# Two of the four opening x tiles move from ScalarE's DMA queue to SyncE's, behind the first two weights

## The chip, the cores and the metric

The kernel runs on one core of a Trainium2 chip. The metric is the device time of one execution in microseconds (us), as the median of several runs. A core has TensorE (PE; its weight loads are shown apart as PEld), VectorE (DVE), ScalarE (ACT), GpSimd (POOL) and SyncE (SP), each with its own instruction stream, and 16 DMA engines that move data between HBM and the on-chip memory. A DMA is issued by an engine's instruction stream; here nearly all are issued by SyncE, and a few by ScalarE.

## The reference

```python
def _A_ref(x, wqkv, wo):          # S = 2048, D = 1024, H = 32 heads
    W, dil = 8, 2
    qkv = (x @ wqkv).reshape(B, S, 3, H, Dh).transpose(2, 0, 3, 1, 4)
    q, k, v = qkv[0], qkv[1], qkv[2]
    # position s attends to s, s-2, ..., s-14 (those that exist)
    ...
    return o.transpose(0, 2, 1, 3).reshape(B, S, D) @ wo

def _B_ref(x, w1, b1, w2, b2):    # F = 3584
    h = jnp.maximum(x @ w1 + b1, 0)
    return (h * h) @ w2 + b2

x = A_x
x = x + _A_ref(_layernorm(x), A_wqkv, A_wo)
x = x + _B_ref(_layernorm(x), B_w1, B_b1, B_w2, B_b2)
x = x + _A_ref(_layernorm(x), A_wqkv, A_wo)
x = x + _B_ref(_layernorm(x), B_w1, B_b1, B_w2, B_b2)
```

Two layers of a dilated sliding-window attention and a dense block with a squared ReLU, both on a layernorm of x, all in bfloat16.

## The kernel before

The 2048 rows are cut into four blocks of 512, a block into four tiles of 128 rows (`tl` 0 to 3). With two layers that makes eight units `u`. The stages of a unit are methods that add operations to a plan: `SA` loads the four x tiles, normalises and transposes them into `xnA`; `SQ` (or `SQ7`, with seven products in place of eight) multiplies by the q, k and v weights; `S2` is the attention, `SW` the output product, `SF1` and `SF2` the dense block. The operations are not emitted as they are added. `Plan.schedule` simulates the engines with a cost for each operation and gives every engine an order, steered by priorities and by three lists of seeds (`ORDER`), and `emit` writes the operations out in that order. Each engine then runs its own stream strictly in order, and waits where an operand is not there.

The opening is unit 0. In `SA(0)` the tiles are taken in the order `ORD = (0, 1, 3, 2)`. Tiles 0 and 1 (x0 and x1 in this text) are issued by SyncE, tiles 3 and 2 (x3 and x2) by ScalarE, since `XACT = (3, 2)`. So "third and fourth" are x3 and then x2.

- x0, x1 and x2 go through `ln_first`: statistics on VectorE (L801, L803), the factor on ScalarE (L794, L795), normalising on VectorE (L798), transposing on TensorE (L817) and a copy into `xnA` by VectorE or ScalarE (L822). For x0 and x1 the transpose and the copy are done in two halves, the first half's copy on VectorE and the second's on ScalarE.
- x3 (`LNA = (3,)`) goes through `ln`: sums on ScalarE (L756 and L760), normalising on VectorE (L769). Its first pass is placed after the factors of x0 and x1 (`after=rst`).
- `keep_clock` (L1559) adds matmuls on constants or on the first normalised tile (`pk`, `pj`) that nobody reads; they occupy TensorE while data are on their way.
- `SQ(0, "kq")` loads the k and q weights in eight pieces of 512 KB on SyncE, alternating k and q; w0 is the first piece of k, w1 the first of q, w2 the second of k, and so on. Its first 16 chunks of matmuls (L909) use only tiles 0 and 1 (256 columns), so they need x0 and x1 transposed and one weight piece each. Tiles 2 and 3 are used later.

On SyncE the order is x0, x1, the eight weight pieces, and then x tiles of the next block (`xt`). Every DMA raises one of eight semaphores when it lands; they are given out in turn, over all queues together, and a DMA that gets a semaphore in use is issued only when the DMA before it on that semaphore has landed.

Of the kernel before, what the change touches and what calls it, by code (L numbers as in the profile page):

```python
# [62 lines left out]
XH = False  # L63
T2 = True
N0 = 4667
XP = -4e5
TAIL = True
CPT = ("xn3",)
# [71 lines left out]
class Plan:  # L140
# [160 lines left out]
    def shift(self, seeds):  # L301

        n = N0 or len(self.ops)
        for s in seeds:
# [21 lines left out]
    def emit(self, place):  # L326
        ndep, left = [o.ndep for o in self.ops], {b: b.left for o in self.ops for b in o.bufs}
        for i, seeds in enumerate(ORDER or [[]]):
            if i:
                for s, o in self.timed:  # L330
                    o.prio = s
                for o, n in zip(self.ops, ndep):
                    o.ndep = n
                for b, n in left.items():
                    b.left, b.slot = n, None
            (self.reshift if i else self.shift)(seeds)
            order, self.timed = self.schedule()
        for o in order:
            for b in o.bufs:
                if b.tile is None:  # L340
                    b.tile = place(b)
            o.fn()

class _Kernel:
# [73 lines left out]
    def place(self, b):  # L418
        pool = self.psum if b.cls == "ps" else self.arena
        return pool.tile(b.shape, b.dt, name=b.tag, tag=f"{b.cls}.{b.slot}", bufs=1)  # L420
# [8 lines left out]
    def dma(self, out, src, r, w, mb, prio=None, after=(), name="dma", cast=None, lat=None, eng="SP", dur=None):  # L429
        def fn():  # L430
            o = out()
            (self.nc.sync if eng == "SP" else self.nc.scalar).dma_start(o if cast is None else o.bitcast(cast), src())
        return self.p.add(eng, dur or 0.08, fn, r, w, self.nxt() if prio is None else prio, after, mb=mb, name=name, lat=lat)

    def par_tile(self, par_ap, t):
# [411 lines left out]
    def SA(self, u):  # L847
# [7 lines left out]
        for tl in ORD if u == 0 else range(4):  # L855
            t = b * 4 + tl
            x, xv = self.load_x(layer, t, after, tag="x0" if u == 0 else "xt", prio=PR1 if u == 1 else (XP if tl in XACT else -1e6) if u == 0 else None,
                                eng="ACT" if u == 0 and tl in XACT else "SP")
# [807 lines left out]
```

## Time and profile before

| | |
|---|---|
| median of 3 runs | 1132.15 us (1131.62 to 1132.54) |
| the profiled execution | 1131.64 us, of which the span from the first to the last instruction is 1129.8 us |
| TensorE busy | 1119.7 us, 99% of the span |
| VectorE busy | 993.9 us, 88% |
| ScalarE busy | 816.6 us, 72% |
| DMA, mean over the span | 321 GB/s |
| mean granted TensorE clock | 1.000 |

The times in the views are us from the span's start. A row of the timeline has start, duration, engine, line, operation with output and inputs, count, and in brackets the idle time of the engine before it and what ended it. A "q" behind an engine's name (SPq, ACTq) is its instruction stream issuing a DMA. In the chain of waits a row has start, length and what the time went to. The table by stage gives for each stretch its length, the busy time (and number of instructions) of each engine, the granted TensorE clock, the share of time that the DMA engines were busy, and GB/s.

### The profile page before, as it was taken

The numbers are of one execution on the slowest core, as the hardware profiler recorded it, in microseconds if no ns is written. First come the engines' busy times: TensorE is split into PE (matmuls) and PEld (weight loads), VectorE is DVE, ScalarE is ACT, GpSimd is POOL, SyncE is SP. The second block draws the span as 40 slices with busy tenths as digits, with TensorE's granted clock in tenths as the row PEclk, the third lists the DMA queues.
The fourth block names the chain that finished last, engine by engine and source line by source line (L and its number), as shares of the span: only waits on it lengthen the run. The fifth ranks groups of instructions, "written<-read, shape, count | busy, mean of one in ns | idle before, by whom it ended". The sixth has DMA issues, their size and how long they took to land.

```text
span 1129.8 us, 20640 instructions
## 1 busy us (share of the span) xinstructions
PE 1119.7 (99%) x7866; PEld 771.5 (68%) x7912; DVE 993.9 (88%) x1530; ACT 816.6 (72%) x1627; POOL 1.8 (0%) x8
## 2 busy tenths in 40 slices
PE   8999999999999999999999999999999999999998
PEld 6645764678846887468864788557884678845864
DVE  8999999999897999959999699996999889996341
ACT  7647897568975799667994669847798477943871
POOL 0000000000000000000000000000000000000000
PEclk9999999999999999999999999999999999999999
DMA  9957889999999986999779998899969999679981
GB/s 355 310 183 240 272 286 334 304 361 383 367 340 382 365 352 245 351 419 355 284 284 317 406 346 319 296 348 374 384 252 333 363 348 394 237 291 339 345 296 68
DMA packets 137021, 362.34 MB, mean 321 GB/s; under 512 B 67418, under 2 KB 68570, under 8 KB 116570
## 3 DMA queue, kind: packets, MB, share of 16 engines
q1 hardware_dynamic: 136490, 360.43, 91.4%
q8 instruction: 62, 1.02, 0.4%
q10 hardware_dynamic: 432, 0.59, 0.1%
q14 instruction: 37, 0.30, 0.1%
HBM read 314.84 MB, written 31.46 MB: 307 GB/s over the span
## 4 chain that ended last, share of the span: by engine, by line
PE 83%; ACT 8%; DVE 5%; DMA 2%; issue 1%; SPq 0%; DVEq 0%; ACTq 0%
PE X L673 22%; PE X L1409 14%; PE Z L673 11%; PE Z L1409 7%; PE Y L673 6%; PE pq L909 5%; PE py L495 4%; PE Y L1409 4%; PE py L1105 3%; PE X L1176 3%; DVE P L979 2%; ACT r L1344 1%; PE Z L1176 1%; ACT rr L1350 1%; DVE P L971 1%
## 5 line engine op out<-in xcount | busy, mean ns | idle before, releaser
L673 PEld LDWEIGHTS <-w 128*128 128x128 f16 (+1 forms) x4904 | 479.6, 98 | 70.4 <-DMA w<-sqv 0.5
L1409 PEld LDWEIGHTS <-r 128*128 128x128 f16 x1162 | 113.7, 98 | 133.4 <-issue 1.5
L1409 PE MATMUL X<-w,r 128*128 128x512 f16 (+1 forms) x763 | 174.1, 379 | 0.6 <-ACT X L508 0.2
L971 DVE TENSOR_TENSOR P<-q,k 128x2048 f16<-128x2048 f16 x128 | 153.4, 1220 | 0.6 <-ACT q L914 0.4
L673 PE MATMUL X<-T,w 128*128 128x256 f16 x1224 | 152.6, 273 | 0.0
L1050 DVE TENSOR_TENSOR pr<-pb,v 128x4096 f16<-128x4096 f16 x64 | 146.0, 2294 | 0.5
L979 DVE TENSOR_TENSOR P<-P,P 128x2048 f16<-128x2048 f16 x110 | 133.5, 1216 | 0.1
L1344 ACT ACTIVATE r<-rr 128x1024 f16<-128x1024 f16 x110 | 122.7, 1133 | 0.5 <-DVE rr L1340 0.4
L1057 DVE TENSOR_TENSOR pr<-pr 128x2048 f16<-128x2048 f16 (+1 forms) x128 | 118.7, 949 | 0.0
L673 PE MATMUL X<-TA,w 128*128 128x256 f16 x864 | 107.9, 273 | 0.0
L909 PE MATMUL pq<-xnA,w 128*128 128x256 f16 (+1 forms) x512 | 86.1, 326 | 1.5 <-ACT k L914 0.8
L606 ACT COPY Y<-X 128x512 f32<-128x512 f32 x115 | 70.1, 609 | 21.0 <-PE X L673 18.3
L1323 ACT CAST y<-Z 128x512 f16<-128x512 f32 x110 | 68.2, 639 | 7.0 <-PE Z L673 6.4
L909 PEld LDWEIGHTS <-w 128*128 128x128 bf16 x512 | 49.9, 98 | 33.1 <-issue 2.1
L1327 DVE TENSOR_TENSOR rr<-u,y 128x512 f16<-128x512 f16 x110 | 45.5, 419 | 26.4 <-ACT u L1313 15.6
L1350 ACT ACTIVATE rr<-Y,b1T 128x256 f16<-128x256 f32 x110 | 53.6, 525 | 4.4 <-PE Y L673 3.6
L673 PE MATMUL X<-xnB,w 128*128 128x256 f16 x440 | 56.0, 273 | 0.0
L673 PE MATMUL Y<-xnB,w 128*128 128x256 f16 x440 | 56.0, 273 | 0.0
L624 ACT CAST u<-X 128x512 f16<-128x512 f32 x72 | 41.8, 585 | 19.2 <-PE X L673 19.2
L1078 ACT CAST yxo<-X 128x512 f16<-128x512 f32 x27 | 15.6, 587 | 55.4 <-PE X L1409 55.4
L1350 ACT ACTIVATE rr<-X,b1T 128x256 f16<-128x256 f32 x110 | 54.7, 546 | 1.2 <-PE X L673 1.1
L628 ACT CAST yq<-Z 128x512 f16<-128x512 f32 x72 | 42.0, 586 | 17.5 <-PE Z L673 17.0
(170 smaller groups left out, 1689.2 us busy)
## 6 DMA issues: line engine op xcount, KB each, us to landing
w<-sw SPq DMA_DIRECT2D x49, 1024.0 KB, 9.7
w<-tw SPq DMA_DIRECT2D x56, 896.0 KB, 6.7
w<-in_B_w_dram SPq DMA_DIRECT2D x42, 896.0 KB, 5.6
w<-in_B_w_dram SPq DMA_DIRECT2D x35, 1024.0 KB, 11.1
w<-in_A_wqkv_dram SPq DMA_DIRECT2D x32, 1024.0 KB, 10.7
w<-sqv SPq DMA_DIRECT2D x24, 1024.0 KB, 11.4
w<-in_B_w_dram SPq DMA_DIRECT2D x28, 512.0 KB, 6.7
w<-sk SPq DMA_DIRECT2D x12, 1024.0 KB, 8.5
```

The lines of the kernel that those rows point to most:

```text
L606: self.p.add("ACT", act(512), lambda: self.nc.scalar.copy(Y[:], X[:]), [(X, 0)], [(Y, 0)], UP, name="u")
L673: nc.tensor.matmul(bank[:, a, :], lw[:, k, a * 128:(a + 1) * 128], rhs(k), start=(start and k == 0 and a == 0), stop=(k == 3), skip_group_ ...
L909: nc.tensor.matmul(pq[:, t0 * HB:t1 * HB], w[:, c0 // 2 % 2, kd // 4, kd % 4, c0 % 2 * 128:c0 % 2 * 128 + 128], xnT[:, 2 * t0:2 * t1, kd, ...
L971: nc.vector.tensor_tensor(cur[:], q[:, c, None, hb * HB:(hb + 1) * HB].to_broadcast([128, W, HB]), _win_ap(k[:, c, :], HALO + hb * HB, HB) ...
L979: nc.vector.tensor_tensor(other[:], other[:], cur[:], ALU.add)
L1050: p.add("DVE", dve(4096), lambda pr=pr, ch=ch: nc.vector.tensor_tensor(pr[:], pb[:].unsqueeze(1).to_broadcast([128, 2, W, HB]), _win_ap2(v ...
L1057: nc.vector.tensor_tensor(dst, pr[:, :, 0:n, :], pr[:, :, n:2 * n, :], ALU.add)
L1323: p.add("ACT", act(512), lambda: nc.scalar.copy(y[:], bank[:]), [(bank, 0)], [(y, 0)], 1.5, name="y")
L1327: p.add("DVE", dve(512), lambda: nc.vector.tensor_tensor(r[:, :, m, :], us[i][:], y[:], ALU.add), [(us[i], 0), (us[i], 1), (y, 0)], [(r, ( ...
L1344: p.add("ACT", 0.955, lambda: nc.scalar.activation(out=r2[:, f:f + 2, :].rearrange("p a t -> p (a t)"), in_=r[:].rearrange("p a m t -> p ( ...
L1350: p.add("ACT", 0.36, lambda a=a: nc.scalar.activation(out=r[:, a, 0, :], in_=bank[:, a, :], func=ACTF.Relu, bias=self.b1T[:, f + a:f + a + ...
L1409: nc.tensor.matmul(banks[q][:, lo:hi], left(jj, q), w[:, j, lo:hi], start=(start and jj == 0), stop=(jj == h - 1), skip_group_check=True)
```

## The change

In the finished order the two x loads that belong to ScalarE are taken out and put back right behind the second weight load, and every x load is issued by SyncE. The plan itself is made as before, with its costs and its order, so all other instructions keep their order on each engine. `B2AT` stands at 0.0 and does nothing. Since semaphores are given out in the order of emission, the first eight DMAs now take them in the order x0, x1, w0, w1, x3, x2, w2, w3 (before: x0, x1, x3, w0, x2, w1, w2, w3).

```diff
+B2AT = 0.0
+XSP = 2
...
             (self.reshift if i else self.shift)(seeds)
             order, self.timed = self.schedule()
+        at = {o: s for s, o in self.timed}
+        if B2AT:
+            b2 = next(o for o in order if o.name == "b2")
+            order.remove(b2)
+            order.insert(next(i for i, o in enumerate(order) if at[o] >= B2AT), b2)
+        if XSP:
+            late = [o for o in order if o.name == "x" and o.eng == "ACT"]
+            ws = [o for o in order if o.name == "w"]
+            order = [o for o in order if o not in late]
+            i = order.index(ws[XSP - 1]) + 1
+            order[i:i] = late
         for o in order:
             for b in o.bufs:
...
-            (self.nc.sync if eng == "SP" else self.nc.scalar).dma_start(o if cast is None else o.bitcast(cast), src())
+            (self.nc.sync if eng == "SP" or XSP and name == "x" else self.nc.scalar).dma_start(o if cast is None else o.bitcast(cast), src())
```

## The prediction

> **What bounds the kernel now.** I began with the page's first lines and with the table of busy time by stage, cut at the points where TensorE stands still: 11.22 us (the end of the opening), 36.23 us and 1120 us.
>
> ```profile
> span 1129.8 us, 20640 instructions
> PE 1119.7 (99%) x7866; PEld 771.5 (68%) x7912; DVE 993.9 (88%) x1530; ACT 816.6 (72%) x1627; POOL 1.8 (0%) x8
> ```
>
> ```profile
> core 0: us, PE busy (x) PEld busy (x) DVE busy (x) ACT busy (x) POOL busy (x), PEclk, DMA share, GB/s
> 0.00:11.22 11.22, 8.17 (x39) 3.54 (x40) 7.44 (x22) 5.66 (x13) 1.76 (x8) 1.00 0.85 322
> 11.22:36.23 25.01, 24.19 (x225) 21.25 (x225) 23.33 (x26) 18.58 (x50) 0.00 (x0) 1.00 1.08 338
> 36.23:1120.00 1083.77, 1080.72 (x7559) 742.49 (x7605) 961.84 (x1481) 790.79 (x1563) 0.00 (x0) 1.00 0.92 323
> ```
>
> TensorE is the bound. It is idle for 11.22 - 8.17 = 3.05 us in the opening, 0.82 us in the next 25 us and 1083.77 - 1080.72 = 3.05 us in all the rest up to 1120 us. The change touches only the opening, so the question is when the first real matmuls start, and whether a shift there reaches the end. The second view is the chain of waits, read forward from its start:
>
> ```profile
> 1.26 4.43 DMA x<-in_A_x_dram
> ...
> 5.71 1.30 DVE st L801 x2
> ...
> 7.81 1.05 ACT xn L756 x2
> ...
> 9.08 0.48 ACT xnA L822
> 9.56 1.14 ACT xn L760 x2
> 10.70 0.48 ACT xnA L822
> ...
> 11.22 2.34 PE pq L909 x20
> ```
>
> It runs: load of x1 (the tile tl = 1), its statistics on VectorE, then ScalarE alone from 7.8 to 11.2 us, then the first long row of matmuls. ScalarE's piece is the first pass of the layernorm of x3 (L756), which stands in ScalarE's order ahead of the two copies that the matmuls wait for. The same stretch in the timeline, with what VectorE and TensorE do beside it:
>
> ```profile
> 4.12 1.29 DVE L801 BATCH_NORM_STATS2 st<-x 128x6 f32<-128x512 bf16 x2 [2.56 <-DMA x<-in_A_x_dram]
> ...
> 7.71 1.35 PE L817 MATMUL pt<-ident,xn 128*128 128x128 f16 x16 [1.13 <-DVE xn L798]
> 7.71 1.04 ACT L756 ACTIVATE xn<-x 128x1024 f16<-128x1024 bf16 x1
> ...
> 8.71 1.28 DVE L801 BATCH_NORM_STATS2 st<-x 128x6 f32<-128x512 bf16 x2
> ...
> 8.90 1.03 PE L1559 MATMUL pj<-xn,ones 128*128 128x512 f16 x4
> ...
> 9.90 0.41 DVE L822 COPY xnA<-pt 128x512 f16<-128x512 f16 x1
> ...
> 10.36 0.60 PE L909 MATMUL pq<-xnA,w 128*128 128x256 f16 x4 [0.43 <-DVE xnA L822]
> ```
>
> L756 at 7.71 reads x3. The statistics at 8.71 read x2, and the copy at 9.90, which releases four matmuls at 10.36, stands behind them on VectorE. So x3 and x2, which are now needed at 7.71 and 8.71 and landed long before, are what the change makes late.
>
> **When each piece lands.** The issues, one by one, in the timeline of the queues, and then the DMA view of the same moments (the last column is us from issue to landing; rows in the order x0, x3, x1, then the first three weights):
>
> ```profile
> 0.80 0.40 SPq L432 DMA_DIRECT2D x<-in_A_x_dram  x1
> 0.83 0.87 ACTq L432 DMA_DIRECT2D x<-in_A_x_dram  x2
> ...
> 1.26 0.41 SPq L432 DMA_DIRECT2D x<-in_A_x_dram  x1
> 1.72 0.43 SPq L432 DMA_DIRECT2D w<-in_A_wqkv_dram  x1
> 2.19 0.43 SPq L432 DMA_DIRECT2D w<-in_A_wqkv_dram  x1
> 2.66 0.46 SPq L432 DMA_DIRECT2D w<-in_A_wqkv_dram  x1
> ...
> 4.11 0.33 SPq L432 DMA_DIRECT2D w<-in_A_wqkv_dram  x1
> 5.71 0.33 SPq L432 DMA_DIRECT2D w<-in_A_wqkv_dram  x1
> ```
>
> ```profile
> x<-in_A_x_dram SPq DMA_DIRECT2D x1, 256.0 KB, 3.3
> x<-in_A_x_dram ACTq DMA_DIRECT2D x1, 256.0 KB, 3.5
> ...
> x<-in_A_x_dram SPq DMA_DIRECT2D x1, 256.0 KB, 4.4
> ...
> w<-in_A_wqkv_dram SPq DMA_DIRECT2D x1, 512.0 KB, 5.4
> ...
> w<-in_A_wqkv_dram SPq DMA_DIRECT2D x1, 512.0 KB, 6.2
> ...
> w<-in_A_wqkv_dram SPq DMA_DIRECT2D x1, 512.0 KB, 7.0
> ```
>
> Issue plus time to landing: x0 0.80 + 3.3 = 4.1, x3 0.83 + 3.5 = 4.3, x1 1.26 + 4.4 = 5.7, weights 1.72 + 5.4 = 7.1, 2.19 + 6.2 = 8.4 and 2.66 + 7.0 = 9.7. The weights land 1.3 us apart, in issue order, so the transfers are bound by bandwidth and 256 KB cost 0.65 us. x0 and x3, issued 0.03 us apart on two queues, land almost together: they share the bandwidth.
>
> **The change, part by part.** It takes two DMA issues off ScalarE's queue and puts both on SyncE's, behind the second weight. The new order on SyncE is x0, x1, w0, w1, x3, x2, w2 and so on.
>
> Removed from ScalarE: 0.87 us of issuing. Between the issue and its first use of data ScalarE waits for VectorE's statistics in any case, so this is worth nothing.
>
> Added to SyncE: two issues of 0.40 and 0.41 us as those of x0 and x1 took, some 0.9 us with their gaps. They delay w2 from 2.66 to about 3.5, and w3 alike. w2's bytes queue behind x2's, which land near 8.2 (below), 4.7 us after w2's issue. From issue to landing with little ahead the nearest row is x0's 3.3 us; less its own 0.65 us and x3's as much, some 2 us are fixed. Since 4.7 is more than that, the issue is hidden behind the backlog. w4 is issued at 4.11, the moment x0 landed, and w5 at 5.71, as x1 landed: SyncE was waiting there for earlier landings, and after the change those two landings are earlier. Without that cover the price would be the 0.9 us itself.
>
> [...]
>
> Gained at the front: x0 no longer shares with x3. It lands 0.65 us before the time at which the pair was through, 4.3 - 0.65 = 3.65; at best a whole piece before its own 4.1, so 3.45. I take 0.55 us earlier (0.45 to 0.65). x1 follows a piece later, at 4.3 instead of 5.7. VectorE's statistics of x0 start at 3.57, those of x1 at 5.71 - 0.55 = 5.16, no longer waiting for a DMA. All up to ScalarE's L756 could then be 0.55 us earlier: ready at 7.16.
>
> Lost behind it: x3 now comes behind x0, x1, w0 and w1. Counted from the front: x1 4.3, w0 5.6, w1 6.9, x3 7.55, x2 8.2. Counted from the back: the bytes up to x2's end are the same as those that were through when w1 landed, 8.4, so x2 lands at 8.4 and x3 at 7.75. Between the two I take 7.65 for x3 and 8.3 for x2. L756 starts at 7.65 plus the 0.02 us between a landing and its reader (x0 landed at 4.1, its reader began at 4.12), thus at 7.67 instead of 7.71: **0.04 us earlier**. The gain of 0.55 us at the front turns into half a microsecond of waiting for x3. The ends: 7.06, if x3 comes in time for a front that is 0.65 earlier, which gives -0.65 us; and 8.4, if x3 is through only with x2, which gives +0.7 us.
>
> From L756 on ScalarE is busy without a break until the copy at 10.70, so the 20 matmuls move by the same 0.04 us, from 11.22 to 11.18. VectorE meets x2 at 8.71 - 0.55 = 8.16 and waits until 8.3; its copy comes at 9.5 instead of 9.90, and the four matmuls at 9.95 instead of 10.36. That gain is lost, since the next 20 wait for ScalarE. TensorE's transposes move from 7.71 to 7.16 and the four fillers (pj) end at 9.4 instead of 9.93; the longest gap is then about 0.6 us, shorter than the 1.13 us that stood before at a granted clock of 1.00, so I put no clock loss into the sum.
>
> **Does the shift reach the end?** The next place where TensorE stands still has these rows (waits of TensorE and SyncE, and timeline):
>
> ```profile
> PE pq L909 <- ACT k L914: 0.8, 1, 0.8
> ...
> SPq L782 <- DMA w<-in_A_wqkv_dram: 3.3, 1, 3.3
> ...
> 21.90 1.24 ACT L735 ACTIVATE xn<-xt,sm 128x1024 f16<-128x1024 bf16 x1
> ...
> 23.16 2.93 SPq L782 DMA_TRANSPOSE xnA<-xn  x1
> ...
> 26.19 1.10 SPq L432 DMA_DIRECT2D xt<-in_A_x_dram  x1
> ...
> 34.53 1.06 ACT L756 ACTIVATE xn<-xt 128x1024 f16<-128x1024 bf16 x1 [2.21 <-DMA xt<-in_A_x_dram]
> ```
>
> At 34.53 ScalarE has waited 2.21 us for a tile xt, and TensorE 0.8 us for ScalarE. That xt was issued at 26.19, behind the transpose at 23.16, which waited for ScalarE's L735 (21.90 + 1.24 = 23.14). So the stop at 36.23 follows ScalarE's pace in the opening, and a shift of 0.04 us passes through it. Afterwards the DMA share stays at 0.92 or more, but TensorE is idle only 3.05 us in 1084, so nothing there absorbs or adds much.
>
> The sum against the profiled execution, which took 1131.64 us for a span of 1129.8 (1.84 us lie around it): 1131.64 - 0.04 = 1131.60. The median of the runs is 0.51 us above that execution, so I forecast 1132.15 - 0.04 = 1132.1.
>
> **The rivals.** A measurement of this kernel can tell about 0.2%, that is 2.26 us, from no change.
>
> *The whole front gain arrives.* x3 lands by 7.1, and the earlier pace also takes off most of the 0.82 us at 36.23: -0.65 to -1.45, so 1130.7 to 1131.5. For it: the front estimate leans early, and SyncE issues w5 sooner. Against: 1.5 MB stand ahead of x3, which at 0.65 us for 256 KB cannot be through by then unless the start-up is shorter than in these rows. 0.09.
>
> *Slower: one queue does not keep the order.* If pieces that stand in one queue share bandwidth with those issued behind them, x3 and x2 land with w2 at 9.7 (L756 2.0 us later, 1134.15) or a weight later, 11.0 (3.3 us later, 1135.4). It decides where x3 lands after 8.4. Against it: the even steps of 1.3 us with several weights outstanding. 0.09, of which 0.05 beyond 0.2%. [...]
>
> *The tile xt comes later.* The transpose at 23.16 and xt behind it meet other traffic; each us later at 34.53 is a us for TensorE. I bound it by ScalarE's wait of 2.21 us doubling: up to +2.2, mostly under 1.5 us, so 1132.6 to 1133.7. 0.08, of which 0.03 beyond 0.2% with other delays.
>
> *SyncE's issue time shows.* [...] If the 0.9 us land on the path through w0 and w1, the result is 1133.0. Against: both weights are issued before the moved tiles. 0.04.
>
> *Nothing moves.* If the two tiles keep their landing times, 1132.15. 0.02.
>
> *Faster for a reason downstream.* A new beat takes away more than 2.26 us out of the 3.87 us that TensorE idles from 11.22 to 1120 us. Nothing in the rows says how. 0.07.
>
> **How the numbers follow.** The forecast keeps 0.61. Its own range is -0.65 to +0.7 us, 1131.5 to 1132.85. Faster by over 0.2%: 0.07. Slower by over 0.2%: 0.05 + 0.03 = 0.08. Within: 0.85. For 8 in 10 the range takes in the first rival, the fourth, and the third up to +1.5 us, and leaves out 0.07 + 0.09 + 0.03: from 1130.6 to 1133.7.
>
> **What would show it.** Right: x0's statistics near 3.6 us instead of 4.12; L756 waiting for the DMA of x, with its start between 7.4 and 7.8; the copy of VectorE earlier by about 0.4 us and the 20 matmuls within 0.3 us of 11.22; SyncE's fifth weight issued when x0 lands. Wrong: L756 starting after 8.4, matmuls of the opening that take longer than 0.12 us each, or a stop at 36.23 that is over 1.5 us or gone.

## The result: slower by some 2.3 us, and the profile after

The changed kernel took 1134.36 us (median of 20 runs, 1132.35 to 1135.72), the kernel before 1131.70 us (20 runs beside them, 1130.62 to 1133.46). The ratio is 1.0020 with a 95% interval of 1.0014 to 1.0026, that is 1.6 to 2.9 us. It lies outside the forecast range (1130.6 to 1133.7).

The runs of the changed kernel fall into two groups by their mean granted clock: 12 at 0.998 with a median of 1134.95 us, 8 at 1.000 with 1133.01 us. So two things are to be explained: a delay of about 1.3 us (1133.01 - 1131.70; 0.7 in the repeat below) that is there in any case, and 1.9 us more in about six runs out of ten. The profiled execution (1135.72 us, the longest of the 20) has both.

Its first lines, and its opening by stage (cut where the granted clock changes):

```profile
span 1134.0 us, 20640 instructions
PE 1122.4 (99%) x7866; PEld 772.5 (68%) x7912; DVE 994.3 (88%) x1530; ACT 815.9 (72%) x1627; POOL 1.8 (0%) x8
```

```profile
core 0: us, PE busy (x) PEld busy (x) DVE busy (x) ACT busy (x) POOL busy (x), PEclk, DMA share, GB/s
0.00:10.31 10.31, 8.35 (x35) 3.39 (x36) 5.01 (x16) 3.23 (x6) 1.76 (x8) 1.00 0.79 270
10.31:13.73 3.42, 1.45 (x12) 1.01 (x12) 3.22 (x7) 3.32 (x12) 0.00 (x0) 1.00 1.02 417
13.73:17.14 3.41, 3.41 (x22) 2.55 (x20) 2.92 (x5) 0.96 (x3) 0.00 (x0) 0.50 1.02 404
```

TensorE works for only 1.45 of 3.42 us in the second row, and in the third the chip grants it half its clock, for 3.41 us. The timeline of the opening says what it waits for:

```profile
3.44 1.29 DVE L814 BATCH_NORM_STATS2 st<-x 128x6 f32<-128x512 bf16 x2 [1.89 <-DMA x<-in_A_x_dram]
...
5.71 1.29 DVE L814 BATCH_NORM_STATS2 st<-x 128x6 f32<-128x512 bf16 x2 [0.74 <-DMA x<-in_A_x_dram]
...
9.36 1.06 ACT L769 ACTIVATE xn<-x 128x1024 f16<-128x1024 bf16 x1 [1.55 <-DMA x<-in_A_x_dram]
...
10.51 1.29 DVE L814 BATCH_NORM_STATS2 st<-x 128x6 f32<-128x512 bf16 x2 [1.72 <-DMA x<-in_A_x_dram]
...
11.72 0.41 DVE L835 COPY xnA<-pt 128x512 f16<-128x512 f16 x1
...
12.18 4.45 PE L922 MATMUL pq<-xnA,w 128*128 128x256 f16 x24 [2.25 <-DVE xnA L835]
12.26 0.57 ACT L835 COPY xnA<-pt 128x512 f16<-128x512 f16 x1
...
13.35 2.79 PEld L922 LDWEIGHTS <-w 128*128 128x128 bf16 x16 [0.15 <-DMA w<-in_A_wqkv_dram]
...
16.42 1.40 PE L830 MATMUL pt<-ident,xn 128*128 128x128 f16 x16
...
17.66 11.52 PE L922 MATMUL pq<-xnA,w 128*128 128x256 f16 x104
```

(The line numbers are 13 higher than before: L769 is the old L756, L814 the old L801, L835 the old L822, L922 the old L909.) x0's statistics start 0.68 us earlier than before (3.44 against 4.12). The gain ends there: those of x1 start at 5.71, as before, now behind a wait for its load. ScalarE waits for x3 until 9.36 (before: 7.71), VectorE for x2 until 10.51 (before: 8.71), each with a copy for the matmuls behind it in its queue. The first matmuls run at 12.18 in place of 10.36, the long row of 104 starts 3.37 us late (17.66; the same row of before stands under the sixth experiment), and the 24 matmuls take 4.45 us, most of them at half clock.

The ninth matmul waits for something else. ScalarE's second copy is done at 12.83 (12.26 + 0.57), but the weight load at 13.35 ends a wait for a DMA: the fourth weight (issued at 4.68, 8.6 us to landing, so 13.3; in the kernel before 3.16 + 7.8 = 11.0). So two things come late at nearly the same time, the copies behind the moved tiles and this weight. In the repeat below it is the copy that ends last, at 13.48, with the weight at 13.4.

The landings, first from the chain of waits (x3), then from the DMA view of the issues at 3.14 us (x2) and at 4.00 us (the third weight), whose last column is us to landing:

```profile
2.67 6.67 DMA x<-in_A_x_dram
```

```profile
x<-in_A_x_dram SPq DMA_DIRECT2D x1, 256.0 KB, 7.3
...
w<-in_A_wqkv_dram SPq DMA_DIRECT2D x1, 512.0 KB, 8.0
```

x3 lands at 9.34, x2 at 3.14 + 7.3 = 10.4 and the third weight at 4.00 + 8.0 = 12.0, where it landed at 9.7 before. The landings keep the order of the issues, but the whole stream is 2.3 us late. The second weight landed at 8.2 (2.19 + 6.0), hardly earlier than before (8.4), though x3 and x2 no longer stood ahead of it. Its rate, over the stretch where the two differ most, up to 9 us and up to the landing of the third weight, first of before, then of after (each with 6 to 9 us as well):

```profile
3.00:6.00 3.00, 3.00 (x11) 1.04 (x9) 1.78 (x4) 0.29 (x1) 0.00 (x0) 1.00 1.05 389
6.00:9.00 3.00, 1.76 (x20) 1.10 (x19) 2.78 (x7) 1.86 (x7) 0.00 (x0) 1.00 1.02 418
...
0.00:9.70 9.70, 7.34 (x35) 3.15 (x36) 5.92 (x18) 4.14 (x10) 1.76 (x8) 1.00 0.82 308
0.00:9.00 9.00, 6.64 (x32) 2.86 (x33) 5.22 (x17) 3.44 (x9) 1.76 (x8) 1.00 0.81 299
```

```profile
3.00:6.00 3.00, 3.00 (x9) 1.06 (x7) 1.78 (x4) 0.50 (x2) 0.00 (x0) 1.00 0.89 293
6.00:9.00 3.00, 2.54 (x21) 1.31 (x20) 2.57 (x6) 0.50 (x2) 0.00 (x0) 1.00 1.03 349
...
0.00:9.00 9.00, 7.42 (x32) 3.10 (x33) 5.01 (x16) 2.28 (x5) 1.76 (x8) 1.00 0.75 252
0.00:12.00 12.00, 8.35 (x35) 3.39 (x36) 6.50 (x19) 4.88 (x10) 1.76 (x8) 1.00 0.82 290
```

From 3 to 6 us the DMA engines move 293 GB/s in place of 389, and from 6 to 9 us still only 349 in place of 418. Up to 9 us that makes 252 x 9 = 2.27 MB in place of 299 x 9 = 2.69, which is 0.42 MB or, at the 404 to 417 GB/s of the later stages above, 1.0 us. The rest is order: up to the third weight's landing 290 x 12.0 = 3.48 MB had moved, before only 308 x 9.7 = 2.99 MB. The pieces issued up to it are the same in both, so 0.49 MB more of later pieces went ahead of its last part, 1.2 us. Together that is the 2.3 us.

### The profile page after: what moved, and what is told of

The parts are those of the page before. It is cut to its first block, busy times and chain, and to the rows that moved or that the text cites. A ratio compares the mean times of both kernels' runs of the same rounds, so it can differ in the third digit from the quotient of the medians.

```text
span 1134.0 us, 20640 instructions
## 1 busy us (share of the span) xinstructions
PE 1122.4 (99%) x7866; PEld 772.5 (68%) x7912; DVE 994.3 (88%) x1530; ACT 815.9 (72%) x1627; POOL 1.8 (0%) x8
## 4 chain that ended last, share of the span: by engine, by line
PE 87%; ACT 6%; DMA 4%; DVE 2%; issue 1%; SPq 0%; ACTq 0%
PE X L686 23%; PE X L1422 14%; PE Z L686 12%; PE pq L922 7%; PE Z L1422 7%; PE Y L686 6%; PE py L508 4%; PE Y L1422 4%; PE X L1189 3%; PE py L1118 3%; ACT r L1357 1%; PE Z L1189 1%; ACT rr L1363 1%; DMA xt<-in_A_x_dram 1%; PE lg L999 1%; DMA w<-in_B_w_dram 1%
## 5 line engine op out<-in xcount | busy, mean ns | idle before, releaser
L922 PE MATMUL pq<-xnA,w 128*128 128x256 f16 (+1 forms) x512 | 87.4, 329 | 2.4 <-DVE xnA L835 2.2
L922 PEld LDWEIGHTS <-w 128*128 128x128 bf16 x512 | 50.4, 99 | 34.5 <-issue 2.8
```

What stands on the lines that cost most here:

```text
L922: nc.tensor.matmul(pq[:, t0 * HB:t1 * HB], w[:, c0 // 2 % 2, kd // 4, kd % 4, c0 % 2 * 128:c0 % 2 * 128 + 128], xnT[:, 2 * t0:2 * t1, kd, ...
```

## The experiments

"Clean" below means the runs whose mean granted clock was 1.000 or 0.999; of the 121 comparison runs of the kernel before, none showed less. Medians are over 7 to 11 runs, those of before over 22 or 33. Intervals are of the ratio to the kernel before on the same chip. Starts are compared by the long row of matmuls behind the transposes (14.29 before, 17.66 after).

**1. The changed kernel once more**, without an edit.

> The changed kernel once more, with a profile of its own. In its first profile x3 landed at 9.34 us and x2 at 10.49, ScalarE's L769 began at 9.36 (7.71 before), TensorE stood still for 2.25 us and its granted clock was 0.5 from 13.7 to 17.1 us. Theory A (the late landing belongs to the new order): L769 again between 9.0 and 9.7 us, a gap of TensorE of about 2 us, time 2.2 to 3 us above the kernel before. Theory B (a chance delay of one DMA engine in that execution): L769 between 7.6 and 8.4 us as predicted, no gap over 1.2 us in this profile.

1133.63 us against 1132.01, 1.0013 (1.0004 to 1.0022). Again the first pass on x3 began late, at 10.01, and again there is a 0.50 row in the clock:

```profile
12.31 0.60 PE L922 MATMUL pq<-xnA,w 128*128 128x256 f16 x4 [2.16 <-DVE xnA L835]
13.53 4.01 PE L922 MATMUL pq<-xnA,w 128*128 128x256 f16 x20 [0.63 <-ACT xnA L835]
```

The row of 20 took 4.01 us where it took 2.34 before. Seven of eleven runs had a clock of 0.998 (median 1134.27), four were clean (1132.69). So the loss and its picture belong to the kernel.

**2. The changed kernel with TensorE kept busy**: each of the four pj fillers is issued three times.

```diff
-                nc.tensor.matmul(pk[:], g, ...)
+                for _ in range(1 if t is None else 3):
+                    nc.tensor.matmul(pk[:], g, ...)
```

> The changed kernel with each of the four filler matmuls pj issued three times (8 more, about 1.7 us of TensorE work that nobody reads, in the gap before the first pq matmuls); plan and all orders as they were. Theory A (about half of the loss is the halved clock that follows the gap): granted clock 1.0 throughout the opening, the first 24 pq matmuls in about 2.9 us instead of 4.45, time 1.0 to 1.7 us below the changed kernel, so 0.9 to 1.7 above the kernel before. Theory C (the late start alone costs the time, the clock nothing): as the changed kernel, within 0.4 us.

1132.49 us, 1.0006 (0.9998 to 1.0015); ten runs of eleven had a clock of 1.000, and the other 0.999.

```profile
8.95 2.75 PE L1573 MATMUL pj<-xn,ones 128*128 128x512 f16 x12
12.73 0.60 PE L922 MATMUL pq<-xnA,w 128*128 128x256 f16 x4 [1.02 <-DVE xnA L835]
13.62 2.34 PE L922 MATMUL pq<-xnA,w 128*128 128x256 f16 x20 [0.30 <-ACT xnA L835]
```

The data come as late as in the first experiment (the first matmul at 12.73), but the 20 matmuls again take 2.34 us. The time falls by 1.1 us (1133.63 - 1132.49; the means differ by 1.1 us as well, with an interval of 0.4 to 1.9): the half clock's share of the median. What stays is 0.5 us, about as in the clean runs of the first experiment (1132.69 - 1132.01 = 0.7).

**3. All four x tiles on SyncE, ahead of the weights.**

```diff
-            i = order.index(ws[XSP - 1]) + 1
+            i = order.index(ws[0])
```

> All four x tiles on SyncE, in front of the first weight (x0, x1, x3, x2, w0, ...). Separates the queue from the place in the order. Theory A (the place behind the weights costs the time): x3 and x2 land by 6.5 us, L769 at 7.7 or earlier, time within 0.5 us of the kernel before. Theory D (four tiles on one queue, in place of two on each, is itself slow, because one DMA engine falls behind): x1 again at about 5.7 us with 15 of 16 parts 0.9 us earlier, x3 and x2 after 7.5 us, time 1 us or more above the kernel before.

1132.55 us, 1.0007 (0.9998 to 1.0015), with the half clock in 4 of 11 runs. Now all x tiles are early, and something else is late:

```profile
9.56 0.60 PE L922 MATMUL pq<-xnA,w 128*128 128x256 f16 x4 [0.44 <-DVE xnA L835]
10.48 0.60 PE L922 MATMUL pq<-xnA,w 128*128 128x256 f16 x4 [0.32 <-ACT xnA L835]
13.00 1.92 PE L922 MATMUL pq<-xnA,w 128*128 128x256 f16 x16 [1.93 <-DMA w<-in_A_wqkv_dram]
```

The first eight matmuls are 0.8 us earlier than before; the ninth waits for the fourth weight until 13.00. This corrects the description of the kernel and the prediction: q's first piece is not the second weight on SyncE but the fourth, and the second chunk of matmuls needs it (its wait ends when the fourth weight lands, here at 4.28 + 8.7 = 13.0). Before, it landed about 1.3 us behind the third, at 11.0, just ahead of the row of 20 at 11.22: a second limit of almost the same height, which the prediction did not see. With all issues on SyncE it is 1.2 to 2.6 us late (after, 1, 2, 3, 10, 11), wherever the x tiles stand.

**4 and 9. Only x3 moved, and only x2 moved.** The other tile stays with ScalarE (the fourth kernel is shown; the ninth has `late[1:2]`; each issue goes by its operation's engine).

```diff
             late = [o for o in order if o.name == "x" and o.eng == "ACT"]
+            late = late[0:1]
+            for o in late:
+                o.eng = "SP"
```

> Only x3 moves to SyncE behind the second weight; x2 stays on ScalarE's queue at the start. Theory A: VectorE's statistics of x2 do not wait, its copy is done by about 10.3 us and the first four pq matmuls start by 10.4; L769 waits for x3 (about 8.7 to 9.4 us) and the next 20 start about 3.5 us after it, 12.2 to 12.9. The loss is then 1 to 1.7 us without the clock, up to 3 with it. Rival E (the loss comes from x2 in front of VectorE's copy, which TensorE's gap of 2.25 us ended on): within 0.5 us of the kernel before.

> Only x2 moves to SyncE behind the second weight; x3 stays on ScalarE's queue. With x3 moved alone the loss was 0.17% (1.9 us), as large as with both. Theory: ScalarE's L773 starts at 7.7 us as before; x2 lands at 9 to 10.5 us and holds VectorE's copy, so the first four pq matmuls start at 10.9 to 12.3 and the 20 right behind; one tile on the second queue, so the third weight lands near 11 as there (9.7 to 10.1 with two tiles on it, 11.7 to 12.3 with none). 0.5 to 1.5 us slower than the kernel before. Rival (x2 alone costs nothing): within 0.3 us.

x3 alone: 1134.10 us, 1.0017 (1.0008 to 1.0026). x2 alone: 1132.27 against 1131.82, 1.0006 (0.9997 to 1.0015). First x3 alone, then x2 alone:

```profile
9.72 1.06 ACT L773 ACTIVATE xn<-x 128x1024 f16<-128x1024 bf16 x1 [1.97 <-DMA x<-in_A_x_dram]
...
13.24 3.80 PE L926 MATMUL pq<-xnA,w 128*128 128x256 f16 x20 [2.33 <-ACT xnA L839]
```

```profile
10.08 1.29 DVE L818 BATCH_NORM_STATS2 st<-x 128x6 f32<-128x512 bf16 x2 [1.42 <-DMA x<-in_A_x_dram]
...
11.75 4.63 PE L926 MATMUL pq<-xnA,w 128*128 128x256 f16 x24 [1.95 <-DVE xnA L839]
```

Either tile stops TensorE by itself, x3 through ScalarE's copies and x2 through VectorE's. Their effects don't add, since the two waits lie beside each other. The half clock came in 7 of 11 and in 3 of 11 runs; in the clean ones the delay was 0.4 us (1132.41 against 1132.01) and 0.1 us (1131.88 against 1131.82).

**5 and 6. The kernel before once more, and with each pj filler issued five times**, which makes the start late at full clock and with unchanged loads.

```diff
+                for _ in range(1 if t is None else 5):
```

> The kernel before once more, with a profile of its own; ratio 1.000 within 0.1%. In the runs so far every order that leaves SyncE's queue alone in the first microseconds moved its bytes late: the piece at the same place in the order of bytes (the third weight) landed at 9.7 us before, at 12.0 and 12.1 in two profiles of the changed kernel. Theory Q (that belongs to the queues): 9.5 to 9.9 us again, first long row of matmuls at 11.0 to 11.5. Rival B (chance of one profile): after 10.5 us here.

> The kernel before with each filler matmul pj issued five times (16 more, about 3.4 us, nobody reads them): DMAs, ScalarE and VectorE as before, no half clock, but TensorE's first pq matmul comes at about 13.3 us and the row of 20 that started at 11.22 starts about 2.1 us later. Prices a late start by itself. Theory L (the start is mostly given back, at the stop that stands at 36.2 us and by what runs ahead meanwhile): 0.3 to 1.0 us slower. Rival (the start passes whole): 1.9 to 2.2 us slower.

Unchanged: 1132.38 us against 1132.42, 0.9998 (0.9989 to 1.0007). With the fillers: 1133.22, 1.0007 (0.9998 to 1.0016). The rows of before, then of the kernel with fillers:

```profile
14.29 11.52 PE L909 MATMUL pq<-xnA,w 128*128 128x256 f16 x104
```

```profile
13.01 2.78 PE L909 MATMUL pq<-xnA,w 128*128 128x256 f16 x24
...
16.52 1.69 PE L909 MATMUL pq<-xnA,w 128*128 128x256 f16 x14
```

A start 2.2 us late (16.52 - 14.29) costs 0.8 us at the end (by the interval up to 1.8), so at least a part, and by the median more than half, is given back. 24 matmuls take 2.78 us here, with all loads on time, and 4.45 us in the changed kernel: 1.67 us is what the half clock adds to them in that profile. Part of what is given back is the stop of TensorE at 36.23 us, 0.82 us in the profile of before: the changed kernel has none there. But the second execution of the unchanged kernel had none either, so it is no fixed reserve.

**7. The first two weights issued by ScalarE, all x by SyncE.**

```diff
+            self.on_act = ws[:2]
...
-            (self.nc.sync if eng == "SP" or XSP and name == "x" else self.nc.scalar).dma_start(...)
+            (self.nc.sync if op[0] not in self.p.on_act and (eng == "SP" or name == "x") else self.nc.scalar).dma_start(...)
```

> All four x tiles on SyncE, as in the changed kernel, but the first two weights are issued by ScalarE instead: two queues work again in the first microseconds, with other tiles on them. Theory Q (a second queue keeps the DMA engines fed): over 330 GB/s from 3 to 6 us, third weight landed by 10.1 us, TensorE's long row by 11.6, time within 0.5 us of the kernel before. Rival R (x tiles on SyncE's queue are slow whatever stands beside them): third weight after 11 us, 0.5 us slower or more.

1133.56 us, 1.0012 (1.0003 to 1.0020). The third weight landed at 10.4, nearly as early as before, but x1 came at 7.3, with the two weights of the other queue beside it, so the matmuls started late all the same. Two queues bring the stream on time here, at 314 GB/s from 3 to 6 us, less than was expected of them. Nine of the eleven runs had a clock of 0.997 or 0.998, and yet they were no slower (median 1133.56) than the two clean ones (1133.35 and 1134.17), one of which is the profiled run. The clock of that profile is dealt with below.

**8. The kernel before with the x tiles cut in halves over both queues** (a switch that the kernel has).

```diff
-XH = False
+XH = True
```

> The kernel before with its switch XH on: x0 and x1 are loaded as two halves of 64 rows, one on each queue, and x3 and x2 follow on ScalarE's queue. Tries for both: x0 without a tile beside it, and two queues. Theory Q: x0's statistics start near 3.6 us and the long row of matmuls up to 0.5 us before 11.22, third weight by 10 us; time 0 to 0.6 us below the kernel before. Rival (splitting costs issue time and the weights come later): 0 to 1 us slower.

1132.38 us, 1.0001 (0.9993 to 1.0010). The third weight landed at 11.9 and the rate from 3 to 6 us was 237 GB/s, with both queues in use. So in this profile a second queue as such does not make the stream fast, which was the reading that the third and seventh experiments had suggested. In the profile, the one run of eleven with a clock of 0.998, x1 came at 6.9 and the first matmuls at 12.82; the other ten runs have a median of 1132.35, as the kernel before. If x1 is 1.2 us late in those too, which no profile shows, it costs nothing there that can be told.

**10. The moved tiles behind the first weight** in place of the second.

```diff
-XSP = 2
+XSP = 1
```

> The changed kernel with XSP = 1: x3 and x2 behind the first weight in place of the second. Theory Q: the stream of bytes is as late as with XSP = 2 (third weight 11.7 to 12.3 us), but x3 stands 512 KB, 1.3 us, further ahead: L769 at 8.0 to 8.8 us, long row of matmuls bounded by the fourth weight (the first of q) at 13.0 to 13.4; TensorE's gap is shorter, so its clock halves less often; 0.5 to 1.3 us slower than before. Rival (place in the order is all): third weight at 9.7 to 10, no more than 0.4 us slower.

1132.66 us, 1.0010 (1.0001 to 1.0019), with the half clock in 2 of 11 runs. x3's first pass began at 7.74, on time, and the fourth weight held the ninth matmul until 12.19. The numbers lie between the third experiment and the changed kernel, as the order does; neither set of expected numbers was met throughout.

**11 and 12. The work on x3 and x2 moved behind the first copies**, in the changed kernel and in the one before (there `ln2` alone of the ScalarE steps), so that a late x tile holds up no copy.

```diff
+        ptc = {e: [o for o in order if o.name == "ptc" and o.eng == e] for e in ("ACT", "DVE")}
+        later([next(o for o in order if o.name == n) for n in ("ln1", "ln2")], ptc["ACT"][1])
+        later([o for o in order if o.name == "bn"][4:6], ptc["DVE"][1])
```

> The changed kernel, with x3's two passes on ScalarE and x2's statistics on VectorE moved behind the copies of x0 and x1 that the first matmuls wait for (nothing else moves). Takes away the standing in line, leaves the late tiles. Theory: the first pq matmuls (8, on the first weight) start by 10.0 us in place of 12.2; the next ones wait for the fourth weight, 13.0 to 13.4; TensorE's clock stays whole more often; x3 is transposed later. 0.5 to 1.2 us below the changed kernel, still 0.3 to 1 above the one before. Rival (x3's and x2's data, not the line, set the time): as the changed kernel within 0.3 us.

> The kernel before, with x3's second pass on ScalarE and x2's statistics on VectorE moved behind those copies. A try for better than both. Expected: first pq matmuls at 9.4 to 9.6 us in place of 10.36, held from the ninth on by the fourth weight (11.0); the transposes of x3 0.2 to 0.5 us earlier at best. Since a start that was 2.1 us later cost only 0.8 us at the end, an earlier one should bring at most 0.3 us: within 0.4 us of the kernel before.

Changed kernel with the edit: 1134.17 us, 1.0017 (1.0008 to 1.0026), no gain; the half clock came in 7 of 11 runs.

```profile
9.50 1.04 PE L930 MATMUL pq<-xnA,w 128*128 128x256 f16 x8
13.14 3.52 PE L930 MATMUL pq<-xnA,w 128*128 128x256 f16 x16 [2.60 <-DMA w<-in_A_wqkv_dram]
```

The first eight matmuls ran 2.7 us earlier than in the changed kernel, and the ninth waited 2.60 us for the fourth weight. The theory that the copies' place behind the late tiles is the whole loss falls: the weight is as late as the tiles, and each of the two is enough (in the fourth experiment it was the copy, which released the matmuls at 13.24, with the weight there by 12.2). Kernel before with the edit: 1132.08 us, 1.0002 (0.9993 to 1.0010); its ninth matmul waited for the same weight until 11.63. No version came out ahead of the kernel before.

**13, 14, 15. A pause in SyncE's issuing.** A store of 32 bytes of x0 is issued by SyncE at one place, so that it goes on only when x0 has landed: behind w1 (13), behind x1 (14, ahead of all weights), behind x2 (15). It went out at 3.43, 3.53 and 3.62 us, where x0's statistics began at 3.44, 3.53 and 3.41. The shortened diff shows the fourteenth; the others have `ws[1]` and `late[1]` for `xs[1]`. The stored line is extra work.

```diff
+            self.probes = {xs[1]: (0, xs[0])}
...
             o.fn()
+            if o in self.probes:
+                to, x = self.probes[o]
+                self.sync.dma_start(self.probe_to[to][:], x.bufs[0].tile[0:1, 0:16])
```

> The changed kernel with a 32-byte store of a part of x0 put on SyncE's queue behind w1: SyncE cannot issue x3 and all that follows before x0 has landed (about 3.5 us in place of 2.67). Theory T (pieces issued into a running queue make its packets long): with four pieces outstanding until 3.5 us, x1 lands by 4.6 us (5.4 to 5.9 so far), over 340 GB/s from 3 to 6 us, third weight by 10.6 us, time 0.5 to 1.5 us below the changed kernel. Rival U (the long packets come whatever is issued): x1 after 5.2 us, under 300 GB/s, third weight after 11.5 us, time as the changed kernel.

> The same store directly behind x1: until x0 has landed only x0 and x1 are outstanding, and no weight. Theory V (the burst comes where the first weight meets the x tiles): x1 lands by 4.4 us, and the long packets come later, when the weights start. Theory T: no burst at all, x1 by 4.4 us. Rival U: x1 after 5.2 us although nothing stands beside it. A hole of about 0.5 us in the stream is the price; third weight 10.5 to 11.5 us under T, after 12 under U.

> The same store behind x2: six pieces outstanding until x0 has landed, w2 after it. Theory T with a depth over six: x1 by 4.6 us, third weight by 10.6. If six are too many already, or under U: x1 after 5.2 us, third weight after 11.5 us, time as the changed kernel.

Behind w1: 1133.27 us against 1132.10, 1.0011 (1.0001 to 1.0021). Behind x1: 1134.82, 1.0027 (1.0016 to 1.0038). Behind x2: 1133.43, 1.0014 (1.0005 to 1.0023). The half clock came in 4 of 10, 7 of 7 and 5 of 10 runs. The third weight landed at 11.8, 12.1 and 12.3, so fewer loads issued at a time did not bring the stream back. The fourteenth separates x1 from the weights: VectorE's rows, and its rate.

```profile
3.53 1.29 DVE L821 BATCH_NORM_STATS2 st<-x 128x6 f32<-128x512 bf16 x2 [1.98 <-DMA x<-in_A_x_dram]
...
4.98 1.23 DVE L821 BATCH_NORM_STATS2 st<-x 128x6 f32<-128x512 bf16 x2
```

```profile
3.00:6.00 3.00, 3.00 (x9) 1.06 (x7) 2.43 (x5) 0.50 (x2) 0.00 (x0) 1.00 0.60 168
```

With no weight behind it x1 landed at 1.25 + 3.2 = 4.45 and was there when VectorE's turn came at 4.98, nearly as the prediction had it (4.3). In the seven profiles where VectorE waits for an x1 with a weight right behind it on SyncE's queue, the wait ends at 5.43 to 5.93 us. The price is the hole in the stream (168 GB/s).

## Why the prediction was wrong

*The front gain.* x0's statistics were put at 3.57 and began at 3.44. This term was right, and it carried nothing: x1, put at 4.3, landed at 5.7. The step took for granted that x1's landing follows from the bytes ahead of it. In the fourteenth experiment, where no weight follows close behind, it nearly did (4.45).

*The landing of x3 and x2.* This is the step that failed: "the bytes up to x2's end are the same as those that were through when w1 landed, 8.4". The bytes asked for are the same; the rate was not, and more bytes of later pieces went ahead. x3 came 1.7 us later than the 7.65 taken, x2 2.1 us later than 8.3. The even steps of 1.3 us from which the rate was drawn are those of the old order from 7 us on (418 GB/s from 6 to 9 us); they did not hold for the new order, neither from 3 to 6 us (293 GB/s) nor from 6 to 9 us (349). The move to the other engine was priced by its issue time alone (0.87 us off ScalarE, some 0.9 us on SyncE, both taken as free); here the issue order and engine together moved the third weight by 2.3 us (9.7 to 12.0), so issue time is not enough to cost such an edit.

*Why the stream is slow* stays open. The runs speak against five single causes, each by one to three profiles: the x tiles' place alone (in the third experiment they come first, and the third weight still lands at 11.7), the lack of a second queue (8), the number of loads outstanding (13, 15), SyncE's time of issuing, and chance (1, 2, 5). On the issuing the prediction was also off: the third weight went out at 4.00 in place of 3.5, and the fifth at 5.18 and not when x0 landed at 3.4, since the issues of x2 and of the third weight took 0.81 and 0.65 us. But in the thirteenth experiment the third weight went out at 4.79 and landed at 11.8, no later than in the changed kernel. The new turn of the semaphores was not tried by itself; the third weight is the seventh DMA in either order, and before the ninth none is seen to wait for a landing (in the kernel before the ninth was issued at 4.11, as the first landed; in the changed one the eleventh at 6.98, as the first weight landed at 6.9). What the fast cases share is that whole x tiles come by one queue and something else by the other from the first issue on: before and its repeats (third weight at 9.7 to 10.3) and, nearly, the seventh (10.4). Against the pattern: one tile on ScalarE's queue gave 11.0 and 11.3 (4, 9), and the tenth, with all on SyncE, 10.9. So it is no cause that was shown.

*The clock.* "I put no clock loss into the sum" is the second failed step: the second experiment puts it at 1.1 us in the median. The reason was wrong too, beyond the size of the gap: the longest idle gap does not tell the profiles apart, since 2.25 us in the changed kernel came with the half clock and 2.94 us in the seventh experiment did not (last section).

*What TensorE needs first.* The chain was read as ScalarE's alone. The fourth weight landed at 11.0, 0.2 us ahead of the end of that chain, as a second limit, and in the third and eleventh experiments and in the profile of the changed kernel it is the last to come.

*Does a shift reach the end?* The prediction let a shift pass whole. A start 2.2 us late cost 0.8 us with an interval up to 1.8 (6), and in the clean runs of the third experiment one that was 1.36 us late (15.65 in its profile) cost nothing that can be told (1131.88 against 1132.01). This error made the result milder.

*The rival on the slow side* gave +2.0 to +3.3 us from x tiles that land with the third weight or later. Its size and direction came out, and its mechanism in part: the landings kept the order of the issues, which it did not expect, but by the sums of bytes above about half of the third weight's delay is that pieces of one queue share bandwidth with those issued behind them. The other half, the lower rate, no rival had.

The sum by the runs: in the clean runs of the changed kernel 1.3 us (0.7 in the repeat), and the half clock in 12 of 20 runs at 1.94 us (1134.95 - 1133.01), which is 1.2 us in the mean: 2.5 us, against a difference of the medians of 2.66 and of the means of 2.36. In the pair of profiles the difference is larger, 1134.0 - 1129.8 = 4.2 us of span; but the repeat of the unchanged kernel had a span of 1130.6, 0.8 us over its first profile, and the changed one fell on its slowest run. So the medians are what is explained here.

## What to carry to other kernels

A rate read from a steady stretch of one order (418 GB/s) did not hold here for the first nine microseconds of another (293 GB/s from 3 to 6 us, 349 from 6 to 9), where loads of 256 and 512 KB stand together: take the landing times of an opening from a run of that order, and don't compute them from bytes. Before a load is moved, list for each of the first matmuls every operand with its landing time, not only the last one in the chain; a second limit 0.2 us from the first (the fourth weight at 11.0, the row of 20 at 11.22) took over in the third and eleventh experiments, where the fourth weight held the ninth matmul until 13.00 and 13.14. And a late operand at the start of this TensorE-bound kernel cost less as time than as idleness: the delay was partly given back (2.2 us late cost 0.8 in the sixth experiment), the half clock in most kernels was not (1.4 to 2.3 us), and eight matmuls that nobody reads (second experiment, all eleven runs at 0.999 or 1.000) bought it off.

## What the hardware showed that was not expected

*The half clock came in single stretches of 3.41 us, each behind one with at most 1.45 us of work.* In the opening of eight of the 17 profiles the granted clock falls to 0.50 for just one stretch of 3.41 us, and the stretch of the same length ahead of it had TensorE busy for 1.45 us or less: 1.45 in the changed kernel (above) and in the ninth experiment, 1.26 in the eighth, 1.09 in the fourth, 0.84 in the first, 0.82 in the eleventh, 0.60 in the fourteenth and fifteenth. Of the ninth:

```profile
9.27:12.69 3.42, 1.45 (x10) 0.80 (x9) 2.61 (x6) 2.22 (x7) 0.00 (x0) 1.00 1.03 422
12.69:16.10 3.41, 3.41 (x19) 2.41 (x17) 3.24 (x6) 1.17 (x5) 0.00 (x0) 0.50 1.02 405
```

In the profiles without such a stretch, a grid of the same length is laid from the start of the trace's clock record. The start lies between 3.9 and 7.1 us, where the fillers go from 0.43 to 0.22 us each, and the record's entries from there on last 3.41 us or a multiple of it (6.83, 3.41 and 1116.2 us in the changed kernel), but for the last, which ends with the run. (Ahead of it the tables show 1.00 as well, but by the fillers' 0.43 us TensorE begins at half pace.) The seventh, which had the longer gap of 2.94 us, and the third:

```profile
1.49:4.90 3.41, 3.41 (x9) 1.18 (x8) 0.05 (x1) 0.58 (x1) 1.33 (x4) 1.00 0.78 255
4.90:8.31 3.41, 1.48 (x7) 0.49 (x5) 2.49 (x5) 0.50 (x2) 0.00 (x0) 1.00 0.98 370
8.31:11.73 3.42, 2.10 (x20) 1.30 (x21) 3.20 (x8) 2.78 (x7) 0.00 (x0) 1.00 1.03 419
```

```profile
11.20:14.61 3.41, 1.61 (x15) 1.45 (x16) 2.90 (x6) 0.71 (x3) 0.00 (x0) 1.00 1.03 418
14.61:18.02 3.41, 3.41 (x41) 3.15 (x40) 3.10 (x4) 2.03 (x4) 0.00 (x0) 1.00 1.03 403
```

In the seventh the border of the grid cut the gap in two; in the third nearly the whole gap of 1.93 us fell into one stretch. No stretch had less than 1.48 us of work, and the clock stayed at 1.00, as in the other seven profiles without a 0.50 row. So in these profiles 1.45 us of work in about 3.41 was followed by the half clock and 1.48 us was not, as far as modelled ends of matmuls can tell figures 0.03 us apart. Where the grid falls differs from one execution to the next (the record of the kernel before starts at 5.32 us in one profile and at 3.92 in the other), and that is the likely reason why the same kernel loses 1.9 us in one run and nothing in another; it was not tried by itself.

What a half-clock stretch costs depends on the kernel. In eight of them its runs lie 1.4 to 2.3 us above the clean ones (medians; 2 to 12 runs with the half clock in each set of runs). In the seventh experiment they do not lie above, and in the eighth the one run lies 0.8 us above. In the eighth's profile the stretch, 8.76 to 12.18 us, was over before the first real matmul at 12.82; for the seventh no run with the half clock was profiled, so its case stays open.

In the changed kernel the stretch ahead of the half clock had work for 42% of its length (1.45 of 3.42 us), and its longest gap was 2.25 us.

*x1 landed later with a weight queued behind it.* x1, 256 KB as the second load of a queue, landed at 4.45 us with nothing behind it (14) and by 4.96 with another x tile behind it (3), where VectorE took it up without a wait; with a weight right behind it VectorE waited for it until 5.43 to 5.93 us in seven profiles (after, 1, 2, 10, 11, 13, 15). The first two rest on one profile each, and in the seventh experiment, with two weights beside it on the other queue, it came at 7.3.
